# Changing how the K and V cache loads of a gated attention decode kernel share one on-chip buffer

## The chip, the cores and the metric

The kernel runs on one NeuronCore of one Trainium2 chip. The metric is the device time of a run in microseconds (us); the time given is the median of several runs.

## What is computed

The reference mixes two blocks with a gate. Block A is attention over a cache for one new token, with 4 batch rows, 32 heads, 8192 cached positions and a head size of 128. Block B is a small gated feed-forward layer for the same token. All tensors are bf16.

```python
def reference(A_x, A_k_cache, A_v_cache, A_wq, A_wo, B_x, B_w_r, B_w_gate, B_w_up, B_w_down, gate_w):
    ...
        q = (lambda x, *d: x.transpose(*d))((x @ wq).reshape(B, Sq, H, Dh), 0, 2, 1, 3)
        scores = jnp.einsum("bhqd,bhkd->bhqk", q, k_cache) * (Dh ** -0.5)
        p = _softmax(scores, axis=-1)
        o = jnp.einsum("bhqk,bhkd->bhqd", p, v_cache)
        return (lambda x, *d: x.transpose(*d))(o, 0, 2, 1, 3).reshape(B, Sq, H * Dh) @ wo
    ...
        g = _silu(x_sel @ w_gate)
        u = x_sel @ w_up
        y = (g * u) @ w_down
    ...
    x = A_x
    g = _sigmoid((x * gate_w).sum(-1, keepdims=True))
    a = _A_ref(x, A_k_cache, A_v_cache, A_wq, A_wo)
    b = _B_ref(x, B_w_r, B_w_gate, B_w_up, B_w_down)
    return g * a + (1 - g) * b
```

The K cache and the V cache are 268 MB each. With the weights, 576 MB are read once.

## The kernel before, in words

**Loads.** Everything large is read through one DMA queue, issued by SyncE (SP) in program order, into one buffer `ring` (L172): five slots of 32 KB in each of the 128 partitions. `load_pair` (L191) takes two slots in a turn that wraps. If they are neighbours, one DMA of 64 KB per partition (8 MB) fills both (L196); if the pair wraps, or if `apart` is asked for, two DMAs of half the size do (L200). The order of the loads is wq, w_gate, K0, K1, w_up, K2 to K8, V0, and then K and V in turn (K9, V1, K10, V2 ...) up to K31. Then come w_down, V23 to V31, and the blocks of wo. A "pair" is four heads of one batch row, so there are 32 of K and 32 of V. V29 to V31 are read in smaller pieces (L569 to L573).

**A K pair** (`k_pair`, L478) is worked off in eight steps: four quarters n (`RD` is 4) and two halves of the head's columns. In each step VectorE transposes 128 x 2048 four-byte words in blocks of 32 x 32 out of the ring into one of three buffers `TB` (L494, buffers given out in turn by `turned`, L179), and TensorE runs eight matmuls on it (L499), which add the scores to `S_ps` in PSUM. Between the steps the program puts other work: at step 2 the sums of a V pair (`flush_sums`, L609, VectorE, for every second V pair), at step 4 the small matmuls that gather them (L625), at step 6 the scaling (L637). Every eighth K pair ends with a softmax (L521 to L535).

**A V pair** (`v_pair`, L559) is 64 matmuls (L579) straight from the ring with the probabilities `PB` as weights. V lags eight pairs behind K.

**The order of the work.** TensorE, VectorE and GpSimd run in the order in which the program is written (`manual_schedule`, L167). A load waits until the last reader of the bytes that it overwrites is done. Before, the last reader of a K quarter is VectorE's transpose; of V and the weights, TensorE.

**The end.** After the last K pair, PSUM is given out anew: `acc` (L661, two banks) gathers the output for both halves of the 1024 columns, `led` (L662) holds small intermediate results. `wd_piece` (L395) loads w_down and multiplies it, `add_x` (L304) adds x, and each `wo_block` (L425) loads a block of wo and later multiplies it (L287, `mm_acc`). Blocks 0 and 1 are loaded ahead of V31, 2 and 3 after it. Blocks 4 to 6 are loaded in halves of 512 KB and the last one in five parts: three of 256 KB and two of 128 KB (L673). At last VectorE (L685) and ScalarE (L687) copy the two halves of `acc` out, and two DMAs store them.

The functions that the change touches, with the profile's line numbers:

Of the kernel before, what the change touches and what calls it, by code (L numbers as in the profile page):

```python
# [8 lines left out]
BF = mybir.dt.bfloat16  # L9
# [103 lines left out]
def kernel(  # L113
# [39 lines left out]
    RING = JR * Dh  # L153
    NS = 5
    assert Sq == 1 and Dh == P and D % P == 0 and F % (P * FR) == 0
# [15 lines left out]

    ring = const.tile([P, NS, RING], BF, name="ring")  # L172
    turn = [0]


    TB = [const.tile([P, CJ * Dh // 2], BF, name=f"TB{i}") for i in range(3)]
    tb_turn = [0]

    def turned(rows, n, dtype=BF):  # L179
        t = TB[tb_turn[0] % 3]  # L180
        tb_turn[0] += 1
        return t[0:rows, 0:n] if dtype == BF else t[0:rows, 0:2 * n].bitcast(dtype)

    def slots(n):
        at = turn[0]
        turn[0] = (at + n) % NS
        return at

    flat = ring[:].rearrange("p s n -> p (s n)")

    def load_pair(src, n, apart=False):  # L191

        a = slots(2)
        if a + 1 < NS and not apart:
            lo = a * RING
            nc.sync.dma_start(out=flat[:, lo:lo + 2 * n], in_=src)  # L196
            return [flat[:, lo:lo + n], flat[:, lo + n:lo + 2 * n]]
        halves = [ring[:, a], ring[:, (a + 1) % NS]]
        for i, half in enumerate(halves):
            nc.sync.dma_start(out=half[:, 0:n], in_=src[:, i * n:(i + 1) * n])  # L200
        return halves

# [12 lines left out]
    N = H * Dh  # L215
    wq_at = load_pair(A_wq.rearrange("(c t) n -> c (t n)", t=DT), DT // 2 * N)
    NX = Bn + 2
# [65 lines left out]
    def acc(n):  # L283
        return A_ps[0][0:Bn, n]

# [69 lines left out]
    def gu_piece(view, w_i):  # L355

        ws = load_pair(view.rearrange("(c t) f -> c (t f)", t=DT), TW * F)

        def cols(w, t, i):
            row = w[:, t * F:t * F + FB].rearrange("p (f m) -> p f m", m=FI)  # L360
            if i < FG - 1:
                return [(0, FR, row[:, :, FR * i:FR * i + FR])]
            return [(0, FR - 1, row[:, :, FR * i:FI]), (FR - 1, FR, w[:, t * F + FB:(t + 1) * F])]
        x_rows(o_ps[w_i], ws, FG, cols)
# [30 lines left out]
    def wd_piece():  # L395
        a = slots(2)
        assert a + 1 < NS and (FI + SX) * D == 2 * RING
        w = flat[:, a * RING:(a + 2) * RING]
        at = FI * D
        nc.sync.dma_start(out=w[:, 0:at], in_=wdv)  # L400
        for u in range(2):
            nc.sync.dma_start(out=w[32 * u:32 * u + 12, at:at + SX * D], in_=wd_apart[u])
        nc.sync.dma_start(out=w[64:72, at:at + D], in_=wd_rest)
        parts = [(hT[:, i // FR, i % FR, :], w[:, i * D:(i + 1) * D]) for i in range(FI)]
        parts += [(hS[:, v, :], w[0:72, at + v * D:at + (v + 1) * D]) for v in range(SX)]
        for i, (lhsT, rows) in enumerate(parts):
            for n in range(NH):
                mm_acc(n, lhsT, rows[:, n * NB:(n + 1) * NB], start=(i == 0))
# [4 lines left out]
    def o_rows(g0, g1):  # L413

        n = g1 - g0
        lp = bank(A_ps[1], 1, [FR, n, Bn])
        for k in range(WB):
# [4 lines left out]

    wo_home = {}

    def wo_block(g, r0=0, r1=FR, half=None):  # L425

        home, at = divmod(g, 4)
        if home not in wo_home:
            wo_home[home] = ring[:, slots(1)].rearrange("p (g r n) -> p g r n", g=4, r=FR)
        w = wo_home[home][:, at]  # L430
        if half is None:
            nc.sync.dma_start(out=w[:, r0:r1].rearrange("p r n -> p (r n)"),
                              in_=wov[:, g, r0:r1].rearrange("p r n -> p (r n)"))
        else:
            nc.sync.dma_start(out=w[:, r0, half * NB:(half + 1) * NB], in_=wov[:, g, r0, half * NB:(half + 1) * NB])

        def use():
            for r in range(r0, r1):
                for n in range(NH) if half is None else [half]:
                    mm_acc(n, LT[:, r, g, :], w[:, r, n * NB:(n + 1) * NB])  # L440
        return use
# [36 lines left out]
    def k_pair(d):  # L478
# [6 lines left out]
        sps = S_ps[g]  # L485
        ks = load_pair(kv_view(A_k_cache, d), RING)
        for n in range(RD):
            kn = ks[n // JT].rearrange("p (c j h m) -> p c h j m", c=JT, h=2, m=Dh // 2)[:, n % JT]
            s = QP - 1 - (RD * t + n)
            for half in range(2):  # L490
                step = 2 * n + half
                flat_t = turned(P, CJ * Dh // 2)
                T = flat_t.rearrange("p (j i e) -> p j i e", j=CJ, e=2)
                nc.vector.transpose(out=flat_t.bitcast(U32).rearrange("p (j i) -> p j i", j=CJ), in_=kn[:, half].bitcast(U32))  # L494
                if step < 2 and ahead:
                    ahead.pop(0)()
                for e in range(2):
                    for z in range(4):
                        nc.tensor.matmul(sps[:, z, :], lhsT=Z[:, 2 * half + e, s:s + P], rhs=T[:, 16 * z:16 * z + 16, :, e],  # L499
                                         start=(t + n + half + e == 0),  # L500
                                         stop=(t == GD - 1 and n == RD - 1 and half + e == 2))
                if step == 2:
# [56 lines left out]
    def v_pair(d):  # L559
# [5 lines left out]
        vv = kv_view(A_v_cache, d)  # L565
        if d < ND - 3:
            vs = load_pair(vv, RING, apart=d >= ND - GD + 2)
        else:
            vs = [ring[:, slots(1)] for _ in range(2)]  # L569
            for half, cuts in ((0, 1), (1, 2)) if d < ND - 1 else ((0, 2), (1, 4)):  # L570
                for c in range(cuts):
                    lo, hi = c * RING // cuts, (c + 1) * RING // cuts
                    nc.sync.dma_start(out=vs[half][:, lo:hi], in_=vv[:, half * RING + lo:half * RING + hi])  # L573
        for u in range(4 * RD):
            n, z = divmod(u, 4)
            vn = vs[n // JT]
# [26 lines left out]
    def sum_up(d, g, t, b, h0):  # L603
# [17 lines left out]
        def finish():  # L621
            ps = A_ps[1] if A_ps else o_ps[1]
            oT = bank(ps, 0, [HV])
# [29 lines left out]
    for kind, d in order:  # L653
        if kind == "k":
# [3 lines left out]
            if d == ND - 1:  # L658
                scores.close()
                fin = ctx.enter_context(tc.tile_pool(name="fin", bufs=1, space=PSUM))  # L660
                A_ps.append(fin.tile([P, NH, NB], F32, name="acc"))  # L661
                A_ps.append(fin.tile([P, 2, NB], F32, name="led"))  # L662
# [9 lines left out]
    last += [wo_block(g) for g in range(2, 4)]  # L672
    cuts = [(g, r, r + 2) for g in range(4, NWB - 1) for r in (0, 2)] + [(NWB - 1, r, r + 1) for r in range(FR - 1)] + [(NWB - 1, 3, 4, n) for n in range(NH)]  # L673
    last += [wo_block(*cut) for cut in cuts]
# [7 lines left out]
    for use in last:  # L682
        use()
    res = [turned(Bn, NB) for _ in range(NH)]
    nc.vector.tensor_copy(out=res[0], in_=acc(0))  # L685
# [33 lines left out]
```

## Time and profile before

| What | Value |
|---|---|
| Time, median of 3 runs | 1342.75 us (1342.62 to 1343.24) |
| The profiled execution: span from its first to its last instruction | 1340.5 us (the page gives no other time of it; the median lies 2.25 us above) |
| Busy: TensorE, VectorE, ScalarE, GpSimd | 1067.9, 638.3, 57.7, 66.6 us |
| Queue of the loads | 575.69 MB, its packets took 99.7% of the span on 16 DMA engines |
| Mean rate | 430 GB/s |
| VectorE waited for K loads ahead of L494 | 463.9 us |
| Last wo piece landed | 1337.04 us |

How to read it: the page gives for each engine the time in which it was busy, then forty slices of the span, then the DMA queues, a chain of work followed back from the end, and groups of instructions. A group's line has its code line, engine, operation, what it writes and reads, and the count; behind the bar stand its busy time, the mean of one in ns, the idle time of the engine just before, and who ended that. A timeline row is start, duration, engine, line and operation; in brackets the idle time before it.

### The profile page before, as it was taken

To read this page: it belongs to the slowest core of one execution; us is meant where nothing else is said; L and a number is where in the kernel's file an instruction comes from. 1 tells how busy PE (TensorE), PEld (TensorE's weight loads), DVE (VectorE), ACT (ScalarE), POOL (GpSimd) and SP (SyncE) were. 2 spreads that over 40 slices of the span, in tenths; PEclk is the share of its full clock that TensorE was granted. 3 is DMA by queue.
4 is the path that set the end of the run, shared out by engine and by line. 5 is a ranking of instruction groups with operands and counts; after the bars stand their busy time and mean duration, and the time that the engine had idled before them with its cause. 6 is when DMAs were issued, how large, how long until landed. Compare 5 with 4: busy or idle time off the path is not lost.

```text
span 1340.5 us, 6937 instructions
## 1 busy us (share of the span) xinstructions
PE 1067.9 (80%) x4654; PEld 141.3 (11%) x1422; DVE 638.3 (48%) x385; ACT 57.7 (4%) x58; POOL 66.6 (5%) x174
## 2 busy tenths in 40 slices
PE   2666878887778788777879778789697879889888
PEld 0101000001011010101001010101011011111111
DVE  2555988556544347554436256646145555100001
ACT  0000000100010000100010000100000000110000
POOL 2000000100010000100010000100001000100000
PEclk9787999898998998898989888899898889889889
DMA  9999999999999999999999999999999999999998
GB/s 415 433 436 435 437 436 424 438 430 430 435 437 426 439 431 428 433 438 431 434 433 433 436 433 438 419 434 431 438 433 441 426 423 435 438 425 430 429 425 348
DMA packets 15512, 576.14 MB, mean 430 GB/s; under 512 B 1740, under 2 KB 2004, under 8 KB 3170
## 3 DMA queue, kind: packets, MB, share of 16 engines
q1 hardware_dynamic: 15474, 575.69, 99.7%
q8 instruction: 24, 0.39, 0.1%
q14 instruction: 6, 0.05, 0.0%
q10 hardware_dynamic: 8, 0.00, 0.0%
HBM read 575.68 MB, written 0.01 MB: 429 GB/s over the span
## 4 chain that ended last, share of the span: by engine, by line
DMA 62%; DVE 22%; PE 13%; another core or an unknown queue 1%; issue 0%; ACT 0%; SPq 0%; DVEq 0%
DMA ring<-in_A_k_cache_dram 51%; DVE TB L494 20%; DMA ring<-in_A_v_cache_dram 9%; PE o_ps L579 8%; PE S_ps L499 2%; PE acc L287 2%; DVE OS L609 2%; DMA x<-in_gate_w_dram 2%; DVE mx L521 0%; PE o_ps L333 0%; PE S_ps L333 0%; PE led L625 0%; DVE PT L535 0%; ACT TB L530 0%
## 5 line engine op out<-in xcount | busy, mean ns | idle before, releaser
L494 DVE STREAM_TRANSPOSE TB<-ring 128x2048 uint32<-128x2048 uint32 x256 | 568.2, 2278 | 471.7 <-DMA ring<-in_A_k_cache_dram 463.9
L499 PE MATMUL S_ps<-TB,Z 128*128 128x512 bf16 x2048 | 531.5, 414 | 186.0 <-DVE TB L494 178.4
L579 PE MATMUL o_ps<-ring,PB 128*64 128x512 bf16 x2048 | 468.5, 392 | 44.9 <-DMA ring<-in_A_v_cache_dram 43.7
L499 PEld LDWEIGHTS <-Z 128*128 128x128 bf16 x512 | 53.0, 103 | 649.6 <-issue 649.6
L579 PEld LDWEIGHTS <-PB 128*64 128x64 bf16 x512 | 57.6, 112 | 447.8 <-issue 443.4
L617 DVE SCALAR_TENSOR_TENSOR OS<-o_ps,mE,OS 128x512 f32<-128x512 f32 x5 | 3.8, 751 | 134.9 <-ACT OS L615 134.9
L476 POOL COPY Z<-qa 32x4 bf16<-32x4 bf16 x128 | 25.6, 200 | 719.2 <-PE S_ps L499 693.2
L555 POOL COPY PB<-PT 32x1024 bf16<-32x1024 bf16 (+3 forms) x23 | 33.3, 1446 | 456.8 <-PE o_ps L579 350.7
L605 ACT ACTIVATE OS<-o_ps,mE 128x512 f32<-128x512 f32 x11 | 7.6, 687 | 673.6 <-PE o_ps L579 673.6
L553 ACT COPY PB<-PT 32x1024 bf16<-32x1024 bf16 (+3 forms) x21 | 30.3, 1443 | 22.3 <-PE o_ps L579 17.3
L609 DVE SCALAR_TENSOR_TENSOR OS<-o_ps,mE,OS 128x512 f32<-128x512 f32 x33 | 24.3, 737 | 1.5
L530 ACT ACTIVATE TB<-S_ps,mx 128x2048 bf16<-128x2048 f32 x4 | 7.9, 1967 | 321.9 <-DVE mx L527 321.9
L287 PE MATMUL acc<-ring,hT 128*4 128x512 bf16 x54 | 14.7, 444 | 5.4 <-ACT TB L530 5.4
L245 PE MATMUL S_ps<-identb,x 6*128 6x6 bf16 x8 | 0.6, 196 | 22.6 <-DMA x<-in_gate_w_dram 22.6
L333 PE MATMUL o_ps<-ring,xw 128*4 128x512 bf16 (+2 forms) x128 | 13.2, 499 | 4.8 <-DMA ring<-in_B_w_gate_dram 4.8
L287 PE MATMUL acc<-ring,LT 128*4 128x512 bf16 x64 | 14.7, 379 | 0.4 <-DVE LT L421 0.4
L625 PEld LDWEIGHTS o_ps<-selg,OS 128*128 128x128 f32 x88 | 11.5, 191 | 9.3 <-issue 8.8
L535 DVE STREAM_TRANSPOSE PT<-TB 128x2048 bf16<-128x2048 bf16 x4 | 9.2, 2312 | 6.4 <-ACT TB L530 6.4
L521 DVE TENSOR_REDUCE mx<-S_ps 128x1 f32<-128x2048 f32 x4 | 9.1, 2282 | 6.2 <-PE S_ps L499 6.2
L625 PE MATMUL o_ps<-selg,OS 128*128 128x8 f32 x88 | 10.5, 245 | 0.0
L637 DVE SCALAR_TENSOR_TENSOR OT<-led,sgb,rinv 128x8 bf16<-128x8 f32 x5 | 1.2, 237 | 18.2 <-PE led L625 18.2
L615 ACT ACTIVATE OS<-o_ps,mE 128x512 f32<-128x512 f32 x5 | 3.4, 687 | 147.9 <-PE o_ps L579 147.9
(83 smaller groups left out, 89.2 us busy)
## 6 DMA issues: line engine op xcount, KB each, us to landing
ring<-in_A_v_cache_dram SPq DMA_DIRECT2D x18, 4096.0 KB, 28.9
ring<-in_A_k_cache_dram SPq DMA_DIRECT2D x14, 4096.0 KB, 33.2
ring<-in_A_v_cache_dram SPq DMA_DIRECT2D x6, 2048.0 KB, 36.7
ring<-in_B_w_gate_dram SPq DMA_DIRECT2D x1, 7168.0 KB
ring<-in_B_w_up_dram SPq DMA_DIRECT2D x1, 7168.0 KB, 37.1
ring<-in_B_w_down_dram SPq DMA_DIRECT2D x1, 6912.0 KB
ring<-in_A_wo_dram SPq DMA_DIRECT2D x4, 1024.0 KB, 32.5
ring<-in_A_v_cache_dram SPq DMA_DIRECT2D x4, 1024.0 KB, 36.0
```

The lines of the kernel that those rows point to most:

```text
L287: nc.tensor.matmul(acc(n), lhsT=lhsT, rhs=rhs, start=start, stop=True, skip_group_check=True)
L333: nc.tensor.matmul(ps[32 * k:32 * k + Bn, z, :].rearrange("p (f r) -> p f r", r=FR)[:, :, lo:hi], lhsT=xT[TW * half + t], rhs=rhs, start=( ...
L476: nc.gpsimd.tensor_copy(out=Z[at, :, QP - 1 + QP * q], in_=qa[at, :, h0 + q, b])
L494: nc.vector.transpose(out=flat_t.bitcast(U32).rearrange("p (j i) -> p j i", j=CJ), in_=kn[:, half].bitcast(U32))
L499: nc.tensor.matmul(sps[:, z, :], lhsT=Z[:, 2 * half + e, s:s + P], rhs=T[:, 16 * z:16 * z + 16, :, e], start=(t + n + half + e == 0), stop ...
L521: nc.vector.tensor_reduce(out=mx[:, 0:1], in_=sps[:].rearrange("p z n -> p (z n)"), axis=AX.X, op=ALU.max)
L535: nc.vector.transpose(out=PT[:].rearrange("p j i -> p (j i)"), in_=PTs)
L553: nc.scalar.copy(out=Bv[at, :, :, q, :], in_=Pv[at])
L555: nc.gpsimd.tensor_copy(out=Bv[at, :, :, q, :], in_=Pv[at])
L579: nc.tensor.matmul(o_ps[w // 2][row:row + NM, w % 2, :], lhsT=PB[:, RD * (d % NW) + n, z].rearrange("p w s j -> p (w s j)"), rhs=vn[:, j0 ...
L609: nc.vector.scalar_tensor_tensor(out=OS[:], in0=o_ps[w // 2][:, w % 2, :], scalar=mE[:, w:w + 1], in1=OS[:], op0=ALU.mult, op1=ALU.add)
L625: nc.tensor.matmul(oT, lhsT=OS[:, q * Dh:(q + 1) * Dh], rhs=selg[:, q].rearrange("p t s -> p (t s)"), start=(q == 0), stop=(q == 3), skip_ ...
```

## The change

The buffer becomes eleven units of 16 KB per partition (`NU`, `UN`) instead of five slots of 32 KB. A pair takes four units. Where it lies is no longer a turn: `plan` lists for each of the 68 loads the first unit and a direction. A pair that begins at unit 9 wraps (9, 10, 0, 1) and is loaded in two halves; all others are one DMA, with fixed cuts for V30 and V31. "UP" works its four units off in rising order, "DOWN" in falling order, K and V alike. V29 is now one DMA.

VectorE transposes K **in place**: L494 reads and writes the same bytes of the ring, and TensorE's matmuls (still L499) read them there. A K unit is then free after its matmuls. The buffers `TB` shrink from three of 8 KB to two of 4 KB, for the other uses.

The two halves of the output get PSUM tiles of their own, at partitions 0 and 32, so that their matmuls use different column tiles of TensorE; the copies at the end write partitions 0 and 32. The wo blocks get fixed places. Blocks 4 to 6 are loaded whole (1 MB; 2 and 3 were already), and the last in three parts of 512, 256 and 256 KB.

The order of the instructions is otherwise the same on every engine, but for the direction within a pair and one more weight load of TensorE for each second output half. Lines of the changed program differ by up to seven from those before: `mm_acc` is L294, K's transposes and matmuls are still L494 and L499, V's matmuls are L572.

```diff
--- before.py
+++ after.py
@@ -151,7 +151,8 @@
     NB = 512
     NH = D // NB
     RING = JR * Dh
-    NS = 5
+    UN = RING // 2
+    NU = 11
     assert Sq == 1 and Dh == P and D % P == 0 and F % (P * FR) == 0
     assert H % GH == 0 and JR == 128 and RD * GD == QP and D % NB == 0
     scale = float(Dh) ** -0.5
@@ -169,36 +170,42 @@
     nc.at_finalize(drop_implied)
     nc.at_finalize(begin_early)
 
-    ring = const.tile([P, NS, RING], BF, name="ring")
-    turn = [0]
-
-
-    TB = [const.tile([P, CJ * Dh // 2], BF, name=f"TB{i}") for i in range(3)]
+    flat = const.tile([P, NU * UN], BF, name="ring")
+
+
+    UP, DOWN = False, True
+    plan = iter([
+        (4, UP), (0, UP), (4, UP), (0, DOWN), (7, UP), (3, UP), (7, UP), (1, UP), (5, DOWN), (0, DOWN), (7, UP), (1, UP),
+        (5, UP), (9, UP), (2, UP), (7, UP), (1, UP), (5, UP), (0, DOWN), (7, UP), (1, UP), (5, DOWN), (0, DOWN), (7, UP),
+        (1, UP), (5, DOWN), (0, DOWN), (7, UP), (3, UP), (7, UP), (1, UP), (5, DOWN), (0, DOWN), (7, UP), (1, UP), (5, DOWN),
+        (0, DOWN), (7, UP), (3, UP), (7, UP), (1, UP), (5, DOWN), (0, DOWN), (7, UP), (1, UP), (5, DOWN), (0, DOWN), (7, UP),
+        (2, UP), (7, UP), (0, UP), (5, UP), (9, UP), (2, UP), (7, UP), (0, UP), (5, UP), (9, UP),
+        (3, UP), (7, UP), (1, UP), (5, DOWN), (0, DOWN), (7, UP), (2, UP), (6, UP), (0, UP), (4, UP)])
+    wo_places = [20, 21, 16, 17, 18, 19, 0, 1]
+
+    TB = [const.tile([P, 4 * NB], BF, name=f"TB{i}") for i in range(2)]
     tb_turn = [0]
 
-    def turned(rows, n, dtype=BF):
-        t = TB[tb_turn[0] % 3]
+    def turned(rows, n, dtype=BF, lo=0):
+        t = TB[tb_turn[0] % 2]
         tb_turn[0] += 1
-        return t[0:rows, 0:n] if dtype == BF else t[0:rows, 0:2 * n].bitcast(dtype)
-
-    def slots(n):
-        at = turn[0]
-        turn[0] = (at + n) % NS
-        return at
-
-    flat = ring[:].rearrange("p s n -> p (s n)")
-
-    def load_pair(src, n, apart=False):
-
-        a = slots(2)
-        if a + 1 < NS and not apart:
-            lo = a * RING
+        return t[lo:lo + rows, 0:n] if dtype == BF else t[lo:lo + rows, 0:2 * n].bitcast(dtype)
+
+    def load_pair(src, n, cuts=(1, 1)):
+
+        place, down = next(plan)
+        lo = place * UN
+        at = [lo, lo + n] if place + 4 <= NU else [lo, 0]
+        assert at[1] or (n == RING and lo + n == NU * UN and not down)
+        halves = [flat[:, x:x + n] for x in at]
+        if cuts == (1, 1) and at[1]:
             nc.sync.dma_start(out=flat[:, lo:lo + 2 * n], in_=src)
-            return [flat[:, lo:lo + n], flat[:, lo + n:lo + 2 * n]]
-        halves = [ring[:, a], ring[:, (a + 1) % NS]]
-        for i, half in enumerate(halves):
-            nc.sync.dma_start(out=half[:, 0:n], in_=src[:, i * n:(i + 1) * n])
-        return halves
+        else:
+            for i, half in enumerate(halves):
+                step = n // cuts[i]
+                for x in range(0, n, step):
+                    nc.sync.dma_start(out=half[:, x:x + step], in_=src[:, i * n + x:i * n + x + step])
+        return halves, list(range(RD))[::-1] if down else list(range(RD))
 
 
     S0 = scp.tile([P, 4, NB], F32, name="S_ps")
@@ -213,7 +220,7 @@
         return b[:, 0:n].rearrange("p (%s) -> p %s" % (" ".join(names), " ".join(names)), **dict(zip(names, shape)))
 
     N = H * Dh
-    wq_at = load_pair(A_wq.rearrange("(c t) n -> c (t n)", t=DT), DT // 2 * N)
+    wq_at, _ = load_pair(A_wq.rearrange("(c t) n -> c (t n)", t=DT), DT // 2 * N)
     NX = Bn + 2
     x6 = const.tile([NX, D], BF)
     nc.sync.dma_start(out=x6[0:Bn], in_=x2)
@@ -281,7 +288,7 @@
     A_ps = []
 
     def acc(n):
-        return A_ps[0][0:Bn, n]
+        return A_ps[n][32 * n:32 * n + Bn]
 
     def mm_acc(n, lhsT, rhs, start=False):
         nc.tensor.matmul(acc(n), lhsT=lhsT, rhs=rhs, start=start, stop=True, skip_group_check=True)
@@ -354,7 +361,7 @@
 
     def gu_piece(view, w_i):
 
-        ws = load_pair(view.rearrange("(c t) f -> c (t f)", t=DT), TW * F)
+        ws, _ = load_pair(view.rearrange("(c t) f -> c (t f)", t=DT), TW * F)
 
         def cols(w, t, i):
             row = w[:, t * F:t * F + FB].rearrange("p (f m) -> p f m", m=FI)
@@ -393,9 +400,9 @@
         nc.vector.tensor_tensor(out=hS[:], in0=hs_ps[0:72], in1=cS[:], op=ALU.mult)
 
     def wd_piece():
-        a = slots(2)
-        assert a + 1 < NS and (FI + SX) * D == 2 * RING
-        w = flat[:, a * RING:(a + 2) * RING]
+        lo = next(plan)[0] * UN
+        assert (FI + SX) * D == 2 * RING and lo + 2 * RING <= NU * UN
+        w = flat[:, lo:lo + 2 * RING]
         at = FI * D
         nc.sync.dma_start(out=w[:, 0:at], in_=wdv)
         for u in range(2):
@@ -413,30 +420,23 @@
     def o_rows(g0, g1):
 
         n = g1 - g0
-        lp = bank(A_ps[1], 1, [FR, n, Bn])
+        lp = bank(A_ps[NH], 1, [FR, n, Bn])
         for k in range(WB):
             for r in range(FR):
                 nc.tensor.matmul(lp[32 * k:32 * k + 32, r], lhsT=identb[:, r:P:FR],
                                  rhs=OT[:, WB * g0 + k:WB * g1:WB, :], start=True, stop=True, skip_group_check=True)
         nc.vector.tensor_copy(out=LT[:, :, g0:g1, :], in_=lp)
 
-    wo_home = {}
-
-    def wo_block(g, r0=0, r1=FR, half=None):
-
-        home, at = divmod(g, 4)
-        if home not in wo_home:
-            wo_home[home] = ring[:, slots(1)].rearrange("p (g r n) -> p g r n", g=4, r=FR)
-        w = wo_home[home][:, at]
-        if half is None:
-            nc.sync.dma_start(out=w[:, r0:r1].rearrange("p r n -> p (r n)"),
-                              in_=wov[:, g, r0:r1].rearrange("p r n -> p (r n)"))
-        else:
-            nc.sync.dma_start(out=w[:, r0, half * NB:(half + 1) * NB], in_=wov[:, g, r0, half * NB:(half + 1) * NB])
+    def wo_block(g, r0=0, r1=FR):
+
+        at = wo_places[g] * FR * D
+        w = flat[:, at:at + FR * D].rearrange("p (r n) -> p r n", r=FR)
+        nc.sync.dma_start(out=w[:, r0:r1].rearrange("p r n -> p (r n)"),
+                          in_=wov[:, g, r0:r1].rearrange("p r n -> p (r n)"))
 
         def use():
             for r in range(r0, r1):
-                for n in range(NH) if half is None else [half]:
+                for n in range(NH):
                     mm_acc(n, LT[:, r, g, :], w[:, r, n * NB:(n + 1) * NB])
         return use
 
@@ -483,22 +483,22 @@
         if t == 0:
             S_ps[g] = S0
         sps = S_ps[g]
-        ks = load_pair(kv_view(A_k_cache, d), RING)
-        for n in range(RD):
-            kn = ks[n // JT].rearrange("p (c j h m) -> p c h j m", c=JT, h=2, m=Dh // 2)[:, n % JT]
+        ks, order = load_pair(kv_view(A_k_cache, d), RING)
+        for k, n in enumerate(order):
+            unit = ks[n // JT][:, (n % JT) * UN:(n % JT + 1) * UN]
+            kn = unit.bitcast(U32).rearrange("p (j h i) -> p h j i", j=CJ, h=2)
+            T = unit.rearrange("p (j h i e) -> p h j i e", j=CJ, h=2, e=2)
             s = QP - 1 - (RD * t + n)
             for half in range(2):
-                step = 2 * n + half
-                flat_t = turned(P, CJ * Dh // 2)
-                T = flat_t.rearrange("p (j i e) -> p j i e", j=CJ, e=2)
-                nc.vector.transpose(out=flat_t.bitcast(U32).rearrange("p (j i) -> p j i", j=CJ), in_=kn[:, half].bitcast(U32))
+                step = 2 * k + half
+                nc.vector.transpose(out=kn[:, half], in_=kn[:, half])
                 if step < 2 and ahead:
                     ahead.pop(0)()
                 for e in range(2):
                     for z in range(4):
-                        nc.tensor.matmul(sps[:, z, :], lhsT=Z[:, 2 * half + e, s:s + P], rhs=T[:, 16 * z:16 * z + 16, :, e],
-                                         start=(t + n + half + e == 0),
-                                         stop=(t == GD - 1 and n == RD - 1 and half + e == 2))
+                        nc.tensor.matmul(sps[:, z, :], lhsT=Z[:, 2 * half + e, s:s + P], rhs=T[:, half, 16 * z:16 * z + 16, :, e],
+                                         start=(t + k + half + e == 0),
+                                         stop=(t == GD - 1 and k == RD - 1 and half + e == 2))
                 if step == 2:
                     flush_sums()
                 if step == RD and d + 1 < ND:
@@ -563,16 +563,9 @@
         row = NM * tv
         flush_sums()
         vv = kv_view(A_v_cache, d)
-        if d < ND - 3:
-            vs = load_pair(vv, RING, apart=d >= ND - GD + 2)
-        else:
-            vs = [ring[:, slots(1)] for _ in range(2)]
-            for half, cuts in ((0, 1), (1, 2)) if d < ND - 1 else ((0, 2), (1, 4)):
-                for c in range(cuts):
-                    lo, hi = c * RING // cuts, (c + 1) * RING // cuts
-                    nc.sync.dma_start(out=vs[half][:, lo:hi], in_=vv[:, half * RING + lo:half * RING + hi])
+        vs, order = load_pair(vv, RING, {ND - 2: (1, 2), ND - 1: (2, 4)}.get(d, (1, 1)))
         for u in range(4 * RD):
-            n, z = divmod(u, 4)
+            n, z = order[u // 4], u % 4
             vn = vs[n // JT]
             for w in range(4):
                 j0 = CJ * (n % JT) + 16 * z + 4 * w
@@ -619,7 +612,7 @@
             nc.vector.tensor_tensor(out=OS[:], in0=half[0], in1=half[1], op=ALU.add)
 
         def finish():
-            ps = A_ps[1] if A_ps else o_ps[1]
+            ps = A_ps[NH] if A_ps else o_ps[1]
             oT = bank(ps, 0, [HV])
             for q in range(4):
                 nc.tensor.matmul(oT, lhsT=OS[:, q * Dh:(q + 1) * Dh], rhs=selg[:, q].rearrange("p t s -> p (t s)"),
@@ -658,7 +651,7 @@
             if d == ND - 1:
                 scores.close()
                 fin = ctx.enter_context(tc.tile_pool(name="fin", bufs=1, space=PSUM))
-                A_ps.append(fin.tile([P, NH, NB], F32, name="acc"))
+                A_ps.extend(fin.tile([P, NB], F32, name=f"acc{n}") for n in range(NH))
                 A_ps.append(fin.tile([P, 2, NB], F32, name="led"))
                 wd_piece()
                 add_x()
@@ -670,7 +663,7 @@
         if (kind, d) == ("v", ND - 2):
             o_rows(0, GE)
     last += [wo_block(g) for g in range(2, 4)]
-    cuts = [(g, r, r + 2) for g in range(4, NWB - 1) for r in (0, 2)] + [(NWB - 1, r, r + 1) for r in range(FR - 1)] + [(NWB - 1, 3, 4, n) for n in range(NH)]
+    cuts = [(g, 0, FR) for g in range(4, NWB - 1)] + [(NWB - 1, 0, 2), (NWB - 1, 2, 3), (NWB - 1, 3, 4)]
     last += [wo_block(*cut) for cut in cuts]
     flush_sums()
     for _ in range(2):
@@ -681,7 +674,7 @@
     o_rows(GE, NWB)
     for use in last:
         use()
-    res = [turned(Bn, NB) for _ in range(NH)]
+    res = [turned(Bn, NB, lo=32 * n) for n in range(NH)]
     nc.vector.tensor_copy(out=res[0], in_=acc(0))
     nc.sync.dma_start(out=out2[:, 0:NB], in_=res[0])
     nc.scalar.copy(out=res[1], in_=acc(1))
```

## The prediction

> **What bounds the kernel now.** I read the page first (span, DMA rows), then the costliest groups, then the timeline of two K pairs, the windows at the start and the chain at the end.
>
> ```profile
> span 1340.5 us, 6937 instructions
> ...
> DMA  9999999999999999999999999999999999999998
> ...
> q1 hardware_dynamic: 15474, 575.69, 99.7%
> ...
> L494 DVE STREAM_TRANSPOSE TB<-ring 128x2048 uint32<-128x2048 uint32 x256 | 568.2, 2278 | 471.7 <-DMA ring<-in_A_k_cache_dram 463.9
> L499 PE MATMUL S_ps<-TB,Z 128*128 128x512 bf16 x2048 | 531.5, 414 | 186.0 <-DVE TB L494 178.4
> L579 PE MATMUL o_ps<-ring,PB 128*64 128x512 bf16 x2048 | 468.5, 392 | 44.9 <-DMA ring<-in_A_v_cache_dram 43.7
> ```
>
> One queue on 16 DMA engines carries 575.69 MB and is busy 99.7% of the span; no slice is idle. VectorE spends 471.7 us waiting, almost all for K. So the time is the sum of the packets, plus any time in which the queue is empty, plus a start and an end. No faster engine can help; what can cost is a load that is issued too late. Two pieces of timeline show how long a K pair occupies its engines once landed, alone (K13) and with the V sums of L609 in between (K14):
>
> ```profile
> 425.11 17.66 DVE L494 STREAM_TRANSPOSE TB<-ring 128x2048 uint32<-128x2048 uint32 x8 [18.62 <-DMA ring<-in_A_k_cache_dram]
> 427.47 17.31 PE L499 MATMUL S_ps<-TB,Z 128*128 128x512 bf16 x64 [5.04 <-DVE TB L494]
> ...
> 444.71 1.48 PE L579 MATMUL o_ps<-ring,PB 128*64 128x512 bf16 x6
> ```
>
> ```profile
> 463.91 6.70 DVE L494 STREAM_TRANSPOSE TB<-ring 128x2048 uint32<-128x2048 uint32 x3 [21.14 <-DMA ring<-in_A_k_cache_dram]
> ...
> 470.53 2.35 DVE L609 SCALAR_TENSOR_TENSOR OS<-o_ps,mE,OS 128x512 f32<-128x512 f32 x3
> ...
> 484.06 1.96 PE L499 MATMUL S_ps<-TB,Z 128*128 128x512 bf16 x8 [0.34 <-DVE TB L494]
> ```
>
> K13 landed at 425.06 and its last matmul ended at 444.71: 19.65 us. K14 landed at 463.86 and ended at 486.02: 22.15 us. A pair takes 19.35 us on the queue (K5, K6 and K7 landed at 173.30, 192.65 and 212.00). Today a ring slot is free when VectorE has copied it out, so a load waits for half a pair (four transposes, 8.9 us); it is issued some 10 us before its turn, and the queue never empties.
>
> **The loads in place.** Number them in SP's order: 0 wq, 1 gate, 2 K0, 3 K1, 4 up, 5 to 11 K2 to K8, 12 V0, then K and V in turn, 57 K31, 58 w_down, then V23 on. Each fills four of eleven units. While load i+1 arrives, i and i+1 hold eight, so load i+2 must take at least one unit of load i. What it costs is set by which one: the first consumed is early, the last consumed means all of load i. In place, "consumed" is after the matmuls, no longer after the transpose.
>
> I walked the 68 entries of the plan. The usual cycle is 7 up, 1 up, 5 down, 0 down. Places 7 and 5 take the first two units of load i; places 1 and 0 the first three. Two units of K: four transposes 8.9, sums 2.35, the last group 1.96, so 13.2 us. Three units of V: TensorE starts it up to 2.8 us after it landed (K14's 22.15 less 19.35) and needs 3/4 of 14.0 (64 matmuls of L579 from 444.71 to 458.71), so 13.3 us. Against 19.35 both leave over 3 us after the delays below, and the two early K loads that take three units (K6, K8: 13.3 + 1.96) leave about 1 us. These cost nothing; their cover is the load ahead of them in the queue.
>
> Five entries break it. They are placed on the unit of load i that is consumed **last**: up at 7 (K0 lies at 4 to 7, upward), K12 at 7 (K11 lies at 5 to 8, upward), and K17, K22 and K27 at 7 (K16, K21 and K26 lie at 7 to 10). In the changed program's order these five wait for the last L499 matmul of K0, K11, K16, K21, K26. SP issues in order, so behind each wait stand all later loads, and nothing else fills the queue.
>
> **The price of one.** Load i's release comes R after it landed (19.65, or 22.15 with sums); SP issues at once (434.03, when the fourth transpose of K13 had ended at 434.01), say 0.05; then the first packets:
>
> ```profile
> 0.00:1.00 1.00, 0.00 (x0) 0.00 (x0) 0.00 (x0) 0.21 (x1) 0.42 (x6) 1.00 0.00 0
> 1.00:2.00 1.00, 0.00 (x0) 0.00 (x0) 0.91 (x1) 1.00 (x1) 0.03 (x1) 1.00 3.20 1049
> ```
>
> SP's first load is issued at 0.00; the last two columns (DMA share, GB/s) are 0 in the first microsecond, and by the packet records the 16 engines begin between 1.01 and 1.43, so 1.15. Last, landing is later than the mean engine's end, as the slowest engine sets it: by the packet records 0.6 us for wq, 1.75 for K0, 1.2 around 450 us, 3.1 at 985. I call it lag. Meanwhile load i+1 kept the queue busy for 19.35. The queue is empty for lag + R + 0.05 + 1.15 - 19.35, which is **lag + 1.5** without sums and **lag + 4.0** with them.
>
> - up: K0, lag 1.75: 3.25.
> - K12 and K22 (no sums fall into K11 and K21): lag 1.2, as an empty queue lines the engines up again and the drift restarts: 2.7 each.
> - K17 (K16 with sums): 5.2. K27 (K26 with sums and one more reciprocal, 20.49 against 20.09 of VectorE): 5.6.
>
> Sum: 19.45 us. With every later lag at 0.6 it is 17.1, with every one at 3.1 it is 27.1.
>
> The Trainium skill, "DMA: Bandwidth & Descriptors", section "Anatomy of one DMA", says that the wait for a semaphore sits on the issuing sequencer before dispatch, and gives an exposed DMA a fixed cost of about 2.0 us; by it (an estimate) the terms would be 2.35 and 4.85, 16.8 in all, 2.7 below my sum. The trace's 1.15 plus 0.6 to 3.1 lies on both sides of that figure, and the trace decides.
>
> **Packets.** Whole pairs replace halves. DMAs over 128 partitions by row size (64, 32, 16, 8, 4, 2, 1 KB): now 47, 32, 6, 8, 6, 3, 2; changed 60, 7, 4, 11, 1, 2, 0. Packets take 2.425, 1.217, 0.629, 0.315, 0.163, 0.085, 0.046 us (packet records), eight per engine and DMA: 1284.6 us now, 1282.9 changed. 17 fewer end marks of 0.009 save 0.15. Together -1.85. Bounds: nothing, or this. A whole pair also lands later than a first half would, but the R above starts at the whole landing.
>
> **The transposes.** In place the reads are the same; the writes go in runs of 128 B instead of one run, and TensorE reads with the same steps. No row shows this transpose in place. Strided writes of VectorE (L347, 128x64 in 192 ns) cost as plain ones (L247, 128x48 in 184), and L609, in place, 737 ns for 512 as L617 into TB takes 743. I take no change (nearest rows). Below: no gain, as 2048 elements take 2278 ns in 4-byte and 2312 in 2-byte form. Above: 10%.
>
> **The end.** The chain:
>
> ```profile
> 1330.33 6.07 PE acc L287 x27
> 1336.41 0.01 issue
> 1336.42 1.05 PE acc L287 x4
> 1337.47 0.02 issue
> 1337.49 0.57 ACT TB L687
> ```
>
> Today TensorE (230 ns per matmul) and the last packets finish together: the last wo piece lands at 1337.04. With two column tiles the pairs may overlap, as the four tiles of L333 do (128 in 13.2 us, 103 ns); then only the last landing counts. Its piece is 256 KB instead of 128: two matmuls side by side instead of one, both copies start together, +0.1. Fewer, larger pieces keep the thinning queue fuller and the engines' lag smaller at the end: 0.5 less (the packet records show 0.9 us lost from 1332 to 1336). If the tiles do not overlap, 2 matmuls in a row add 0.2. The w_down matmuls (54, 14.7 us) lie beside V23's load. I take -0.4.
>
> **Sum** against the profiled execution's span of 1340.5: +19.45 - 1.85 - 0.4 = +17.2, so 1357.7. The median of the runs, 1342.75, lies 2.25 above the span; the same 2.25 gives **1360.0 us**.
>
> **Rivals.**
> - *The five waits are covered after all*: a K pair is done before its successor's transfer ends. The place is the last unit of K0, K11, K16, K21, K26; the price is 0 instead of 19.45; it decides where R falls under 19.35 - 1.2 - 1.2 = 16.95, a transpose pitch of 1.85 us instead of 2.21. Then 1342.75 - 2.25 = 1340.5, not slower. Against it: the pitch follows the element count, and K13 in the trace needed 19.65.
> - *In-place transposes are slower*: 10% adds 1.8 us to each R, 9 us in the five gaps: 1369; at 20% the three-unit places open too, 1380 and more. For it: no row shows one.
> - *The change does less than it says*: the tiles do not overlap, TensorE ends after the DMA. Price 0.2 to 1 us; it hides in the range.
>
> **How the numbers follow.** Five gaps as priced: 0.82, from 1356 (lag 0.6 for K0 too, 16.0, and first packets after 1.01 instead of 1.15, 0.7 less) to 1368 (lag 3.1). Slower transposes: 0.09, 1365 to 1380. Waits covered: 0.09, 1340.5, which is 0.17% below the median, so split 0.06 within 0.2% and 0.03 faster. (0.2%, 2.7 us, is about what a measurement of this kernel can tell from no change.) Range 1353 to 1370: the first case with its bounds, 2.1 less than its lowest if up's wait alone were covered (lag 0.6), and some of the second.
>
> **What would show it.** In the changed profile: DMA tenths and GB/s dip in the slices near 80, 370, 570, 760 and 960 us; among SP's waits five loads wait for PE L499 and their K or up lands about 22 us after issue instead of 30; VectorE's transposes stay at 2278 ns; the DMA sum falls by some 2 us. It is wrong if the transposes change, if those five loads are issued before the queue runs out, or if further dips appear at the other K loads.

## The result, and the profile after

| | Before | After |
|---|---|---|
| Time, median | 1342.99 us (1342.62 to 1343.41, 4 runs) | 1367.5 us (1366.14 to 1368.44, 4 runs) |
| Ratio, 95% interval | | 1.0181 [1.0169, 1.0194] |
| Span of the profiled execution | 1340.5 us | 1366.6 us (time of this run 1368.44) |

The change costs 24.5 us where 17.2 were forecast. The page of the changed kernel, with the lines that answer to those of before:

```profile
span 1366.6 us, 6942 instructions
...
DMA  9989999999899999899999899999899999999998
GB/s 434 424 370 438 442 432 430 428 432 432 376 430 430 447 434 432 346 430 434 445 426 438 376 430 430 432 439 444 344 428 430 432 430 430 441 419 430 430 419 350
...
q1 hardware_dynamic: 12738, 575.69, 97.9%
...
L494 DVE STREAM_TRANSPOSE ring<-ring 128x2048 uint32<-128x2048 uint32 x256 | 567.9, 2278 | 493.7 <-DMA ring<-in_A_k_cache_dram 493.7
L499 PE MATMUL S_ps<-ring,Z 128*128 128x512 bf16 x2048 | 527.3, 412 | 240.1 <-DVE ring L494 232.6
L572 PE MATMUL o_ps<-ring,PB 128*64 128x512 bf16 x2048 | 463.2, 389 | 35.3 <-DMA ring<-in_A_v_cache_dram 34.1
```

A slice is 34.2 us. Slices 3, 11, 17, 23 and 29 are no longer full: they hold 68 to 102, 342 to 376, 547 to 581, 752 to 786 and 957 to 991 us, the five places of the forecast. (Slice 40 is the end.) The transpose takes 2278 ns in place as it did into TB. VectorE waits 30 us more for K with its own work unchanged: that follows a queue that ran dry. TensorE waits 54 us more for VectorE; how much of that is the queue, no run tells apart.

One of the five, K12, in the timeline (start, duration, engine, line; in brackets the idle time before):

```profile
352.90 17.66 DVE L494 STREAM_TRANSPOSE ring<-ring 128x2048 uint32<-128x2048 uint32 x8 [18.22 <-DMA ring<-in_A_k_cache_dram]
...
370.62 1.89 PE L499 MATMUL S_ps<-ring,Z 128*128 128x512 bf16 x8 [0.30 <-DVE ring L494]
...
372.54 0.33 SPq L202 DMA_DIRECT2D ring<-in_A_k_cache_dram  x1
...
395.61 4.50 DVE L494 STREAM_TRANSPOSE ring<-ring 128x2048 uint32<-128x2048 uint32 x2 [25.05 <-DMA ring<-in_A_k_cache_dram]
```

K11 landed at 352.88; its last matmul ends at 372.51 and SP issues K12 at 372.54. V3, the only load that was queued meanwhile, was done by then. The windows of the same stretch (the last two columns are DMA share and GB/s):

```profile
371.00:372.00 1.00, 1.00 (x6) 0.10 (x1) 0.00 (x0) 0.00 (x0) 0.00 (x0) 1.00 0.00 0
372.00:373.00 1.00, 1.00 (x6) 0.11 (x1) 0.00 (x0) 0.00 (x0) 0.00 (x0) 1.00 0.00 0
373.00:374.00 1.00, 1.00 (x7) 0.13 (x2) 0.00 (x0) 0.00 (x0) 0.00 (x0) 1.00 2.77 918
374.00:375.00 1.00, 1.00 (x6) 0.20 (x2) 0.00 (x0) 0.00 (x0) 0.00 (x0) 1.00 0.34 131
```

A window books a packet where it starts, so 2.77 says only that nearly all 16 engines restarted in that microsecond. By the packet records they start between 373.50 and 374.29, 1.15 us after the issue on average. These first packets of 64 KB take 2.68 to 3.51 us, mean 3.11, where the others take 2.42 (median). From the mean engine's end of V3 (370.16) to that of K12 (393.80) it is 23.64 us, 4.29 more than the 19.35 of a pair. I call this excess the gap of a load. The gaps of the changed kernel:

| Load | Forecast, us | Measured, us | Lag of the load waited for: forecast, measured |
|---|---|---|---|
| w_up | 3.25 | 4.27 | 1.75, 2.0 |
| K12 | 2.7 | 4.29 | 1.2, 2.15 |
| K17 | 5.2 | 6.35 | 1.2, 1.77 |
| K22 | 2.7 | 3.84 | 1.2, 1.7 |
| K27 | 5.6 | 6.72 | 1.2, 1.75 |
| V26 | 0 | 1.39 | no gap expected |
| Sum | 19.45 | 26.86 | |

### The profile page after: what moved, and what is told of

Same layout as the page of the kernel before. It is cut to its first block, busy times and chain, and to the rows that moved or that the text cites. A ratio compares the mean times of both kernels' runs of the same rounds, so it can differ in the third digit from the quotient of the medians.

```text
span 1366.6 us, 6942 instructions
## 1 busy us (share of the span) xinstructions
PE 1046.3 (77%) x4654; PEld 142.8 (10%) x1486; DVE 638.0 (47%) x385; ACT 57.5 (4%) x58; POOL 66.4 (5%) x174
## 4 chain that ended last, share of the span: by engine, by line
DMA 64%; DVE 18%; PE 17%; issue 0%; ACT 0%; SPq 0%; DVEq 0%
DMA ring<-in_A_k_cache_dram 50%; DVE ring L494 16%; PE S_ps L499 11%; DMA ring<-in_A_v_cache_dram 9%; PE o_ps L572 5%; DMA ring<-in_B_w_gate_dram 3%; DVE OS L602 2%; DMA ring<-in_A_wo_dram 1%; PE acc L294 1%; PE o_ps L340 1%; DVE mx L521 0%; PE led L618 0%; DVE PT L535 0%; ACT TB L530 0%; DVE TB L678 0%
## 5 line engine op out<-in xcount | busy, mean ns | idle before, releaser
L494 DVE STREAM_TRANSPOSE ring<-ring 128x2048 uint32<-128x2048 uint32 x256 | 567.9, 2278 | 493.7 <-DMA ring<-in_A_k_cache_dram 493.7
L499 PE MATMUL S_ps<-ring,Z 128*128 128x512 bf16 x2048 | 527.3, 412 | 240.1 <-DVE ring L494 232.6
L572 PE MATMUL o_ps<-ring,PB 128*64 128x512 bf16 x2048 | 463.2, 389 | 35.3 <-DMA ring<-in_A_v_cache_dram 34.1
L499 PEld LDWEIGHTS <-Z 128*128 128x128 bf16 x512 | 53.5, 105 | 700.5 <-issue 700.5
L572 PEld LDWEIGHTS <-PB 128*64 128x64 bf16 x512 | 57.3, 112 | 432.1 <-issue 425.0
L294 PE MATMUL acc<-ring,hT 128*4 128x512 bf16 x54 | 8.4, 486 | 5.4 <-ACT TB L530 5.4
L618 PEld LDWEIGHTS o_ps<-selg,OS 128*128 128x128 f32 x88 | 11.5, 191 | 8.9 <-issue 8.6
L294 PE MATMUL acc<-ring,LT 128*4 128x512 bf16 x64 | 8.9, 394 | 3.4 <-DMA ring<-in_A_wo_dram 2.9
L618 PE MATMUL o_ps<-selg,OS 128*128 128x8 f32 x88 | 10.5, 245 | 0.0
```

Source lines behind the costliest of these rows:

```text
L294: nc.tensor.matmul(acc(n), lhsT=lhsT, rhs=rhs, start=start, stop=True, skip_group_check=True)
L494: nc.vector.transpose(out=kn[:, half], in_=kn[:, half])
L572: nc.tensor.matmul(o_ps[w // 2][row:row + NM, w % 2, :], lhsT=PB[:, RD * (d % NW) + n, z].rearrange("p w s j -> p (w s j)"), rhs=vn[:, j0 ...
L618: nc.tensor.matmul(oT, lhsT=OS[:, q * Dh:(q + 1) * Dh], rhs=selg[:, q].rearrange("p t s -> p (t s)"), start=(q == 0), stop=(q == 3), skip_ ...
```

## The experiments

The theory: the five loads that the plan puts on the last consumed unit of K0, K11, K16, K21 and K26 cost all of the difference, by the gap each leaves in the queue. The rivals: something general costs (eleven small units, in-place transposes, whole pairs), or the end does. "Before" beside the experiments has a median of 1342.89 to 1342.96 us in 15 to 33 runs.

**Keep the plan, but load five K pairs as halves**, so that the load after the next can start when the first half has been read:

```diff
-        if cuts == (1, 1) and at[1]:
+        if cuts == (1, 1) and at[1] and not apart:
...
-        ks, order = load_pair(kv_view(A_k_cache, d), RING)
+        ks, order = load_pair(kv_view(A_k_cache, d), RING, apart=d in (0, 11, 16, 21, 26))
```

> The changed kernel with its plan untouched, but the five K pairs whose last unit is waited for (K0, K11, K16, K21, K26) are loaded as two halves. Theory (place): those five waits for a whole K pair cost 25.4 us (4.3, 4.3, 6.3, 3.8, 6.7 by the packet records of the changed run). With a half landing 9.7 us earlier the transposes start earlier, the release comes about 11 us after the pair has landed instead of 19.7 or 22.2, and all five go: about 1342.5 us, five halves cost 0.4, and only the short gap near 1222 us stays. Rival (in place itself): a unit is free only after its matmuls, wherever it lies, so about 1367. Rival (end): the column tiles or the larger wo pieces cost the time, so about 1367.

Measured: 1344.3 us (1342.54 to 1345.23), ratio to before 1.0007 [0.9998, 1.0016]. SP issues K12 11 us earlier than in the changed kernel (there at 372.54), before the queue runs out:

```profile
361.37 0.33 SPq L202 DMA_DIRECT2D ring<-in_A_k_cache_dram  x1
```

No gap over 0.5 us is left, not even the one near 1222 us that was expected to stay. Five DMAs cut in two take back 23 of the 24.5 us. The expected 1342.5 lies just under the interval, which begins at 1342.7; the 1.8 us above it are not explained.

**Another plan**, in which each load takes only the first one or two consumed units of the load before the last. Only the list changes: (4, UP), (0, UP), (7, UP), (1, UP), (5, UP), (9, UP) ... with 15 pairs that wrap.

> The changed kernel with another list of places and directions: every load takes only the first one or two consumed units of the load two before it (where it would take three of V it is moved), 15 wraps instead of 3. Everything else is the changed kernel. Theory (place): no gap at all, also not near 1222 us; packets 1.85 less than before the change and 1.0 more for twelve further wraps, the end 0.4 less: about 1341.7 us, a little under the kernel before. Rival (in place itself): about 1367. Rival (end): about 1367.

Measured: 1342.92 us, ratio 0.9998 [0.9989, 1.0007], no gaps before the last blocks. So units, in-place transposes and the new end together cost nothing that can be measured (the interval is -1.5 to +0.9 us), and the places are the whole loss: those of the five loads, and V26's, which this plan moves too. The theory holds. Two things are not settled here. The gain that was expected besides (1341.7 us) did not come. And e2 loads about as much in whole pieces (48 DMAs of 64 KB per partition) as the kernel before (47; the changed kernel 60), so on the rival of whole pairs only e1 speaks, with 55 of them at 1344.3 us.

**In-place transposes in the old ring**:

```diff
...
-                nc.vector.transpose(out=flat_t.bitcast(U32).rearrange("p (j i) -> p j i", j=CJ), in_=kn[:, half].bitcast(U32))
+                nc.vector.transpose(out=kn[:, half], in_=kn[:, half])
...
```

(The lines left out shape the views, so that L500, here the matmuls, reads the ring.)

> The kernel before with one part of the change alone: K transposed in place in its ring of five slots; loads, cuts and end as before. Theory (place): a load here waits for half a pair; that wait ends about 2 us later and the queue had some 10 us in hand, so 1343.0, the same within 0.5 us. Rival (in place itself): most of the 24.5 us, 1360 or more. Transposes at 2278 ns as in both kernels.

Measured: 1344.89 us, ratio 1.0013 [1.0004, 1.0022]: 1.9 us over before, where the same within 0.5 us was expected. The transposes take the same time (2278 ns); one load is late:

```profile
249.03 0.33 SPq L197 DMA_DIRECT2D ring<-in_A_k_cache_dram  x1
```

This is K9. In the kernel before it was issued at 245.86. K8 starts behind the first softmax, so its matmuls are late (and TensorE was granted 0.50 of its clock from 236 to 244 us), and in place it is they that free the slot. The gap it leaves is 1.76 us. So later release alone has a price where the cover is thin.

**The end alone**, in the kernel before: column tiles, PSUM tiles and the new cuts of wo.

```diff
...
-        return A_ps[0][0:Bn, n]
+        return A_ps[n][32 * n:32 * n + Bn]
...
-    cuts = [(g, r, r + 2) for g in range(4, NWB - 1) for r in (0, 2)] + [(NWB - 1, r, r + 1) for r in range(FR - 1)] + [(NWB - 1, 3, 4, n) for n in range(NH)]
+    cuts = [(g, 0, FR) for g in range(4, NWB - 1)] + [(NWB - 1, 0, 2), (NWB - 1, 2, 3), (NWB - 1, 3, 4)]
```

> The kernel before with the end of the change alone: column tiles, PSUM tiles of their own, wo blocks 4 to 6 whole and the last in three parts. Theory (place): nothing of the 24.5 us is here; 0.4 less for packets and end marks and about 0.4 less at the end, 1342.2. Rival (end): slower, up to 1367.

Measured: 1343.44 us, ratio 1.0004 [0.9995, 1.0012]. The gain is missing; the runs of the last blocks below show why.

**One word of the plan**: K11 worked off downward, so K12 takes its first two units.

```diff
-        (5, UP), (9, UP), (2, UP), (7, UP), (1, UP), (5, UP), (0, DOWN), (7, UP), (1, UP), (5, DOWN), (0, DOWN), (7, UP),
+        (5, UP), (9, UP), (2, UP), (7, UP), (1, UP), (5, DOWN), (0, DOWN), (7, UP), (1, UP), (5, DOWN), (0, DOWN), (7, UP),
```

> The changed kernel with one word of the plan turned: K11 at units 5 to 8 is worked off downward, so that K12 at 7 takes its first two units. Theory (each of the five loads costs its own gap, and gaps add): only K12's gap of 4.29 us (packet records) goes, 1367.5 - 4.3 = 1363.2 us, and its dip near 372 us is gone. Rival (the five gaps share one cause upstream, or a later load pays what an earlier one saves): 1366 to 1368.

Measured: 1363.37 us (1362.34 to 1364.48), ratio to before 1.0154 [1.0140, 1.0168]: 4.1 us less than after, as expected. The gaps of the other four loads stay (3.92, 5.94, 3.92, 6.68). V26's gap is not there in the profiled execution of this run, nor in that of the next one, and between the profiled executions the difference to after is 6.1 us; so the agreement of the medians to 0.2 us is closer than these few runs can show.

**Only K16 and K26 as halves**: the edit of e1 with (16, 26).

> The changed kernel with K16 and K26 alone loaded as two halves, the two whose pair holds the V sums. Theory: the two dear gaps go (6.35 and 6.72 us, 13.07 together), the halves cost 0.1 each: 1354.6 us; the three gaps at 4.3, 4.3 and 3.8 stay. If the sums were not what makes a gap dear, and all five cost alike (25.4 / 5 = 5.1 each): 1357.3.

Measured: 1353.8 us (1352.42 to 1354.88), ratio 1.0080 [1.0067, 1.0092]. The two gaps with V sums were worth some 13.7 us (V26's may be in it), not twice 5.1: the 2.35 us of sums within the K pair are part of the price, as the gaps of the changed kernel show too (6.35 and 6.72 with sums, 3.84 to 4.29 without).

**Seven more places turned the wrong way**: K5, K13, K15, K18, K20, K23 and K25 from (5, DOWN) to (5, UP).

> The changed kernel with seven more words of the plan turned the wrong way: K5, K13, K15, K18, K20, K23 and K25 at units 5 to 8 are worked off upward, so that the load after the next waits for the last matmul of each. Theory: seven gaps more, five without sums at 4.1 us (mean of up, K12, K22 as measured) and two with sums (K18, K20) at 6.5: 33.5, so 1401 us. By the prediction's sizes (2.7 and 5.2 to 5.6) it would be 24, so 1392. If gaps overlap or saturate: under 1385.

Measured: 1396.45 us, ratio 1.0398 [1.0384, 1.0412]: 28.95 us over after for seven gaps, between the forecasts. The page:

```profile
span 1394.9 us, 6942 instructions
...
GB/s 425 438 371 448 424 393 421 448 425 425 387 431 440 391 422 393 361 423 420 391 421 359 393 421 421 391 447 365 361 450 423 427 440 428 435 431 436 429 417 350
```

There are now twelve dips. Each slice at 393 or less holds one, but for the last. The seven new gaps are 3.92, 4.00, 4.00, 5.42, 6.50, 4.10 and 4.10, 32.0 in all; V26's gap is not there, and K17's and K27's are 1.1 and 0.6 shorter. K17 shows why. K16 now follows a gap itself, its lag is 0.64 in place of 1.77, and K17's gap is 5.24 in place of 6.35: 1.13 less lag, 1.11 less gap. So in this pair of loads the lag counts with its full size.

Five of the versions, in their profiled executions (their time less 1342.9):

| Kernel | Gaps | Sum of the gaps, us | Time above 1342.9, us |
|---|---|---|---|
| e2, other plan | 0 | 0 | 0.05 |
| e6 | 3 | 11.5 | 10.9 |
| e5 | 4 | 20.5 | 19.4 |
| after | 6 | 26.9 | 25.5 |
| e7 | 12 | 55.7 | 53.8 |

Gaps add, and each costs the time some 0.2 us less than the mean engine's excess. A reading that fits and was not tried by itself: the end goes by the slowest engines, which were late anyway and lose less.

**Smaller last pieces** in the other plan without gaps: the last wo block in five parts, as before.

```diff
-    cuts = [(g, 0, FR) for g in range(4, NWB - 1)] + [(NWB - 1, 0, 2), (NWB - 1, 2, 3), (NWB - 1, 3, 4)]
+    cuts = [(g, 0, FR) for g in range(4, NWB - 1)] + [(NWB - 1, r, r + 1) for r in range(FR - 1)] + [(NWB - 1, 3, 4, n) for n in range(NH)]
```

> The other plan without gaps (e2_replan), with the last wo block in five parts as before (three of 256 KB, two of 128 KB), blocks 4 to 6 whole and the column tiles kept. Theory (the end is set by the last landing, and a smaller last piece leaves one matmul and less data behind it): 0.1 to 0.4 us under e2_replan, 1342.5 to 1342.8 us. Rival (five small parts lose at the end of the queue what they save after it): 1342.9 to 1343.3.

Measured: 1342.14 us (1341.87 to 1343.03, 11 runs), and once more:

> e8_replan_small_last once more, beside e9 and e10 on the same chip: 1342.1 us, copy at 1338.0, clock 0.5 to 0.6 in the last 4 us.

1342.22 us (1342.00 to 1343.03, 11 runs). The second agrees with what was expected of it; the first is 0.4 us under its forecast. But the ranges overlap with the other plan's (1342.19 to 1343.09), whose runs fall into two groups as these do: four of eleven under 1342.5 us, seven at 1342.9 or more. So the difference of the medians, 0.7 to 0.8 us, says mostly which group a median fell into. TensorE's rows at the end of e8 tell more:

```profile
1331.88 1.03 PE L289 MATMUL acc<-ring,LT 128*4 128x512 bf16 x8 [1.46 <-DMA ring<-in_A_wo_dram]
1334.36 3.58 PE L289 MATMUL acc<-ring,LT 128*4 128x512 bf16 x16 [1.45 <-DMA ring<-in_A_wo_dram]
```

Eight matmuls on two column tiles take 1.03 us; the last sixteen take 3.58, not 2.1. The windows of the same kernel say why (the third column from the end is the granted clock):

```profile
1332.00:1334.00 2.00, 0.91 (x8) 0.26 (x5) 0.00 (x0) 0.00 (x0) 0.00 (x0) 1.00 0.79 308
1334.00:1336.00 2.00, 1.64 (x8) 0.50 (x9) 0.00 (x0) 0.00 (x0) 0.00 (x0) 0.60 0.64 240
1336.00:1338.00 2.00, 1.94 (x10) 0.41 (x6) 0.03 (x1) 0.00 (x1) 0.00 (x0) 0.55 0.06 21
```

With the column tiles TensorE is done early, idles for the blocks, and is granted 0.55 to 0.60 of its clock just when the last block comes. So the end waits for TensorE again. To test that, **fifteen matmuls that nobody reads** fill its idle time:

```diff
-    for use in last:
+    for use, n in zip(last, (3, 6, 6, 0, 0, 0, 0, 0)):
+        for i in range(n):
+            nc.tensor.matmul(A_ps[NH][0:Bn, 0], lhsT=LT[:, 0, 0, :], rhs=flat[:, (64 + i) * NB * 2:((64 + i) * 2 + 1) * NB], start=True, stop=True, skip_group_check=True)
```

> e8_replan_small_last with fifteen matmuls of TensorE whose result nobody reads (3 ahead of wo block 4, 6 ahead of 5, 6 ahead of 6, into the unused half of led), so that TensorE doesn't idle between the last blocks. Theory (in e8 TensorE idled 1.46 us ahead of block 6, was granted 0.6 and then 0.55, and the last 16 matmuls took 3.58 us in place of some 2): granted clock 1.00 from 1334 to 1338, block 6 starts no later, the copy starts about 0.8 us earlier, at 1337.1 in place of 1337.98; time 1341.3 us against e8's 1342.1. Rival (the clock isn't set by what TensorE did in the microseconds before, or the last landing at about 1336.8 sets the end): the copy starts within 0.2 us of e8's, and the added matmuls may delay it.

Measured: 1342.13 us (1341.91 to 1342.41, 11 runs); ratio to before 0.9993 [0.9984, 1.0002]. The last windows:

```profile
1334.00:1336.00 2.00, 2.00 (x17) 0.50 (x10) 0.00 (x0) 0.00 (x0) 0.00 (x0) 1.00 0.63 229
1336.00:1338.00 2.00, 1.29 (x9) 0.42 (x6) 0.68 (x1) 0.58 (x1) 0.00 (x0) 1.00 0.05 18
```

The clock stays at 1.00 and the copy starts at 1337.31 in place of 1337.98. The median is the same all the same: of the 22 runs of e8 and e11 ten lie above 1342.5 us and twelve at 1341.9 to 1342.2, and the profiled ones are among the ten. Of e9's eleven none lies above 1342.5. A reading that fits: whether the clock falls before the last block differs from run to run, and filling the idle time takes that away, and no more. None of the twelve was profiled, so that their clock stayed up is not shown. The expected 0.8 us were those of an unlucky run.

**No column tiles**, else as e8:

```diff
...
-        return A_ps[n][32 * n:32 * n + Bn]
+        return A_ps[n][0:Bn]
...
```

> e8_replan_small_last with both output halves on the same column tile again (partition 0 for both, the PSUM tiles stay apart). Theory (the column tiles make TensorE idle, and the idling costs the clock): 16 matmuls at 230 ns follow each other with little idle time, clock 1.00, the copy starts at 1337.3 to 1337.6, as in the kernel before (1337.49); time 1341.7 us, between e9_busy_end and e8. Rival (the tiles are what makes the end short): the copy starts after 1338.0 and the time is over e8's by up to 1 us.

Measured: 1344.93 us, ratio 1.0014 [1.0005, 1.0023]: 2.7 us over e11, and my theory of it missed. The clock did stay at 1.00. But V24 waits for the last matmul of w_down and is now issued at 1158.99 in place of 1151.79, and the gap it leaves is 1.87; and the last 31 matmuls follow each other at 230 ns until 1339.5, after the packets. With this plan the column tiles are needed ahead of V24.

## Why the prediction was right, and what was mis-sized

*The mechanism* was right. The five loads named wait for L499 of K0, K11, K16, K21 and K26, and the dips and e1, e2, e5, e6 and e7 agree. SP's longest waits, in the kernel before (first row) and in the changed one (us in total, times, longest):

```profile
SPq L196 <- DVE TB L494: 458.6, 25, 28.8
...
SPq L202 <- PE S_ps L499: 661.4, 30, 37.2
```

*"Waits covered"* fell: K12 left its gap, and e5 won its 4.1 us. *"In-place transposes slower"* fell: 2278 ns in after and in e3. *"Does less than it says"* was half right: the column tiles overlap (16 matmuls in 1.89 us, 118 ns each, 230 before), yet the end gained nothing.

*The price of one* was too low, by two terms:

- The lag. I let it fall to 1.2 after a gap, on the ground that an empty queue lines the engines up. At the end of K17 the slowest engine is 0.40 us behind the mean, at the end of K12 one engine of the 16 is still 1.35 behind, and by the load that is waited for next the lag is 1.7 to 2.15. Over the five this is +2.8 us (0.25, 0.95, 0.57, 0.5 and 0.55). The range's upper bound, a lag of 3.1 for every later load, covered it.
- The restart. The 1.15 us to the first packet was about right (1.15 to 1.3 in the five), but the first packets are slower: at K12 3.11 us in place of 2.42. At the five gaps this is 0.79, 0.69, 0.61, 0.57 and 0.62 us, +3.3 in all. The trace of before had it, and I missed it: wq, the first load, took 20.1 us on its engines where a pair takes 19.35.

With both, K12 is 2.7 + 0.95 + 0.7 = 4.35 against 4.29. The Trainium skill, "DMA: Bandwidth & Descriptors", section "Anatomy of one DMA", puts the wait for a semaphore on the issuing sequencer, which K12 shows; its fixed cost of about 2.0 us would stand for 1.15 + 0.7 + the lag, which is 3.4 to 4.0 us here. The section fits that cost to DMAs issued by GpSimd, which the prediction did not say; these are issued by SP.

*V26* was costed at nothing, as a three-unit place with over 3 us to spare, and left 1.39. V24's units were consumed late, since TensorE was at half clock when V24 had landed:

```profile
1200.00:1205.00 5.00, 3.04 (x15) 0.33 (x3) 1.60 (x3) 2.33 (x4) 1.21 (x2) 1.00 1.12 485
1205.00:1210.00 5.00, 3.75 (x9) 0.54 (x4) 0.50 (x1) 0.06 (x1) 0.00 (x0) 0.51 1.03 446
1210.00:1215.00 5.00, 5.00 (x17) 2.03 (x11) 0.24 (x1) 0.00 (x0) 0.00 (x0) 0.50 1.03 446
```

Its first eight matmuls took 3.59 us and the gathering L618 1.88. In e1 the same pair came after the same idle time (3.45 us against 3.21) at full clock, took 1.89 and 1.06, and V26 left no gap:

```profile
1180.00:1185.00 5.00, 3.64 (x20) 1.40 (x12) 0.61 (x2) 0.00 (x0) 0.00 (x0) 1.00 1.06 459
```

*Packets and end*, -1.85 and -0.4, did not reach the time. In e2, with a dozen more pairs in halves than after, the packets took 0.75 us less per engine than before, and the median is the same. In the changed kernel the packets took 2.3 us more per engine than before, where 2 less were forecast: the slow first packets add more than the whole pairs save. (The forecast counts 17 end marks fewer; by its own list of DMAs it is 19, 0.02 us more.) At the end TensorE's clock can take back what the tiles give: e4's last sixteen matmuls took 3.58 us, as e8's did.

*The sum*: 19.45 + 2.8 + 3.3 + 1.39 gives 26.9, as measured, of which the time shows 25.5 in the profiled execution and 24.5 in the median. That 1367.5 us still lies under the 1368 of the first case is partly luck: the bound was made for the lag alone, which took 2.8 of the 7.7 us that it allowed, and the slow first packets, V26 and the savings that did not come used up the rest.

## What to carry to other kernels

When a buffer is freed by a later engine than before, list for every load which unit it takes and when that unit's last reader ends, and compare it with the end of the one transfer that still covers it; a single pair worked off in the other direction was worth 4.1 us here. Price a queue that runs dry with three things beside the wait: the slowest engine's lag, the time to the first packet, and the slower first packets. Of a cover that is TensorE's work, subtract what half its clock would cost.

## What the runs showed of the hardware that I had not expected

- The first packets after the queue was empty are 0.6 to 0.8 us longer (at K12 3.11 against 2.42 us for 64 KB).
- A DMA in two halves costs next to nothing while the queue is full: in the kernel before the two halves of V0 took the mean engine 9.71 us each, 19.42 together, a whole pair 19.35.
- TensorE's clock fell to 0.50 to 0.60 after idle stretches of no more than 1.5 us with busy ones of 1 us between (e8, e11), and once did and once did not after one of 3.2 to 3.5 us (after, e1). The Trainium skill, "TensorE: Matmul & The Clock Gate", section "What's actually happening", has a window of some 3.4 us that runs by itself, so that the moment differs from run to run; the ten of 22 runs would fit that. Its section "HAM oscillation — how this bites in real kernels" allows idle gaps up to the window; e8 shows the clock falling at shorter ones.
